# Sharing softmax exponentials between ScalarE and VectorE, and issuing score matmuls more than once

## The chip, the cores and the metric

The kernel runs on one core of a Trainium2 chip. The metric is device time in microseconds of one execution. The engines are TensorE (PE, matmuls), ScalarE (ACT, activations), VectorE (DVE), GpSimd (POOL) and the DMA queues. "Granted clock" is the share of the full TensorE clock that was let through.

## The reference, cut to what matters

```python
# S = 2048 tokens, D = 640, H = 32 heads of Dh = 20, F = 1536
def _A_ref(x, wqkv, wo):                 # attention
    q, k, v = ...                        # x @ wqkv, split into heads
    scores = jnp.einsum("bhqd,bhkd->bhqk", q, k) * (Dh ** -0.5)
    p = _softmax(scores, axis=-1)
    o = jnp.einsum("bhqk,bhkd->bhqd", p, v)
    return o_as_rows @ wo
def _B_ref(x, w1, b1, w2, b2):           # MLP over tokens
    h = _layernorm(x, axis=-1)
    ...
x = x + _A_ref(_layernorm(x), A_wqkv, A_wo)
x = x + _B_ref(_layernorm(x), B_w1, B_b1, B_w2, B_b2)    # layer norm of a layer norm
# ... and both lines once more
```

Per layer 32 heads x 2048 x 2048 exponentials have to be computed, which is 134 million, against 20-column heads that give the matmuls little work.

## The kernel before

Scores are computed transposed, in chunks of 128 keys by 512 queries of one head. Three chunks make a tile of three PSUM banks, and ACT does one exponential over the whole tile. Four heads form a group (64 chunks), and their P V products are accumulated in one bank. Work for other stages (projections, part of the MLP) is "filling": it is issued to PE between tiles.

```python
sps = p1.enter_context(tc.tile_pool(name=f"sps{layer}", bufs=2, space=PSUM))
...
def emit_S(t):
    cs = chunks[3 * t:3 * t + 3]
    ...
    St = sps.tile([128, 3, 512], F32, name="S")
    S_tiles[t] = St
    for i, (n, j) in enumerate(cs):
        s_matmul(St, i, n, j)            # 32-row matmul at row position 32*j

def emit_exp(t):
    ...
    P = ptp.tile([128, 3, 512], BF16, name="P")
    nc.scalar.activation(out=P[:, 0:ncs, :]..., in_=St[:, 0:ncs, :]..., func=ACT.Exp, scale=SCALE)

def emit_PV(n):                          # four chunks, column positions 0, 32, 64, 96
    ...
...
for t in range(NTILES):
    if t + 1 < NTILES:
        emit_S(t + 1)
    emit_exp(t)
    n_pv = 0
    while pv_done < NU and (4 * pv_done + 3) // 3 <= t - LAGT:
        emit_PV(pv_done)
        ...
    emit_fills(CFG["FILL_PV"] if n_pv else CFG["FILL_NOPV"], misc_alloc)
```

The layer norm of a layer norm is done as written, statistics and application twice:

```python
mean, rstd = ln_stats(x1s[:])
t1 = lnw.tile([128, D], F32, name="ln_t1")
ln_apply(t1[:], x1s[:], mean, rstd, engine="dve")
mean2, rstd2 = ln_stats(t1[:])
ln_apply(h2t[:], t1[:], mean2, rstd2, engine="dve")
```

The softmax here doesn't subtract the row's maximum and nothing guards it: scores larger than these inputs give would overflow.

## Time and profile before

Before the prediction there were five runs: median 2176.28 us, 2174.34 to 2180.15.

| stage | from, us | to, us | length, us |
|---|---|---|---|
| prologue | 0 | 50.03 | 50 |
| attention 1 | 50.03 | 1005.68 | 955.7 |
| MLP 1, projections of layer 2 | 1005.68 | 1130.30 | 125 |
| attention 2 | 1130.30 | 2081.30 | 951.0 |
| MLP 2 | 2081.30 | 2174.5 | 93 |

The view of stretches gives the busy time of each engine in the first attention stage of the kernel before (the second has the same, within 1 us for each engine). Its columns are: the stretch, its length, then PE, weight loads, DVE, ACT and POOL busy (with instruction counts), the granted clock, the DMA share and GB/s.

```profile
50.03:1005.68 955.65, 774.35 (x4913) 218.43 (x4912) 216.69 (x423) 927.43 (x683) 67.71 (x96) 0.74 0.12 27
```

ACT is busy for 927 of 956 us and DVE for 217; the granted clock averages 0.74. PE's busy time is measured at a low clock, and the same matmuls take longer there: a group of three score matmuls lasts 0.39 us at 99.80 us, at full clock, and 0.61 at 101.16, at half clock.

### The profile page before, as it was taken

The page shows a single profiled execution, that of the slowest core. Times are in us where ns is not written, and L with a number is a line of the kernel's source. Part 1 is how long each engine was busy: PE and PEld are TensorE (multiplying, and loading weights), DVE is VectorE, ACT ScalarE, POOL GpSimd, SP SyncE. Part 2 cuts the span into 40 slices and gives each one's busy share as a digit, 9 for nine tenths or more (in the row PEclk, how much of TensorE's full clock was granted, in tenths as well). Part 3 has the DMA queues.
Part 4 walks back from the last instruction along what each step waited for, and adds up shares of the span by engine and source line. Part 5 has one row for each costly group of instructions (what it writes and reads, how often), then busy time and mean ns, then how long its engine had stood idle before and what let it go on. Part 6 is the DMA issues. An engine that isn't in the chain of part 4 may idle for free.

```text
span 2174.5 us, 28088 instructions
## 1 busy us (share of the span) xinstructions
PE 1765.4 (81%) x11360; PEld 558.9 (26%) x11360; DVE 584.0 (27%) x1255; ACT 1949.7 (90%) x1508; POOL 166.8 (8%) x250
## 2 busy tenths in 40 slices
PE   7788887777878789886997778788778877898869
PEld 4222222222222122222542222222222221222225
DVE  6112123211421032213642111322123210422242
ACT  5999999999999999995449999999999999999952
POOL 2000000110012001110000000001000110111000
PEclk9877788985887575665999888877668875765569
DMA  5000000110024002223620000101100330122145
GB/s 125 1 1 1 1 10 28 48 63 7 31 56 61 8 28 40 38 31 87 225 84 1 1 1 1 37 20 57 46 25 25 67 57 1 55 47 35 19 135 176
DMA packets 90723, 96.64 MB, mean 44 GB/s; under 512 B 9696, under 2 KB 68192, under 8 KB 90592
## 3 DMA queue, kind: packets, MB, share of 16 engines
q1 hardware_dynamic: 70464, 71.22, 10.5%
q0 software_dynamic: 20128, 23.62, 6.8%
q8 instruction: 89, 1.46, 0.3%
q14 instruction: 42, 0.34, 0.0%
HBM read 55.48 MB, written 39.32 MB: 44 GB/s over the span
## 4 chain that ended last, share of the span: by engine, by line
ACT 43%; PE 32%; issue 21%; DVE 3%; DMA 1%; POOL 0%; ACTq 0%; SPq 0%; DVEq 0%; POOLq 0%
ACT P L312 42%; PE S L293 9%; PE acc L518 5%; PE misc L217 4%; PE y L704 4%; PE misc L393 3%; PE misc L420 2%; PE pp L208 2%; PE misc L453 1%; PE big L633 1%; DMA ua<-uacc 1%; DVE bnst L152 0%; DVE bnst L153 0%; POOL rstd L159 0%; PE pp L217 0%
## 5 line engine op out<-in xcount | busy, mean ns | idle before, releaser
L312 ACT ACTIVATE P<-S 128x1536 bf16<-128x1536 f32 (+1 forms) x1366 | 1854.7, 1538 | 53.0 <-PE S L293 41.8
L293 PE MATMUL S<-QTq,KT 32*128 32x512 bf16 x4096 | 671.4, 481 | 353.2 <-ACT P L312 333.9
L518 PE MATMUL acc<-P,Vaug 128*32 128x512 bf16 x4096 | 513.8, 491 | 5.3 <-DVE T L321 4.1
L293 PEld LDWEIGHTS <-KT 32*128 32x128 bf16 x4096 | 215.8, 94 | 895.2 <-issue 870.6
L518 PEld LDWEIGHTS <-Vaug 128*32 128x32 bf16 x4096 | 111.6, 97 | 336.7 <-issue 336.7
L399 DVE COPY ustg<-misc 128x512 f32<-128x512 f32 (+1 forms) x144 | 70.4, 489 | 348.8 <-PE misc L393 344.3
L393 PE MATMUL misc<-h2st,w1st 128*128 128x512 bf16 (+1 forms) x576 | 155.6, 384 | 0.1
L321 DVE STREAM_TRANSPOSE T<-acc 128x512 f32<-128x512 f32 x64 | 45.8, 716 | 390.8 <-PE acc L518 390.7
L159 POOL TENSOR_TENSOR rstd<-veps,mhalf 128x1 f32<-128x1 f32 x96 | 54.0, 563 | 1222.4 <-DVE veps L157 1195.3
L404 POOL DMA_DIRECT2D uacc<-ustg x96 | 83.0, 866 | 485.6 <-DVE ustg L399 448.2
L217 PE MATMUL misc<-hh,wq_pad 128*128 128x512 bf16 x310 | 119.7, 459 | 0.0
L704 PE MATMUL y<-uT,w2s 128*128 128x512 bf16 (+1 forms) x768 | 107.6, 299 | 2.9 <-ACT uT L647 2.8
L480 DVE CAST QTq<-misc 128x512 bf16<-128x512 f32 x62 | 42.8, 691 | 245.9 <-PE misc L217 245.9
L217 PE MATMUL misc<-hh,wk_pad 128*128 128x512 bf16 x280 | 108.6, 469 | 0.0
L480 DVE CAST KT<-misc 128x512 bf16<-128x512 f32 x56 | 38.7, 691 | 230.8 <-PE misc L217 230.8
L420 PE MATMUL misc<-wo_pad,attnT 128*128 128x512 bf16 (+1 forms) x384 | 95.7, 358 | 0.0
L704 PEld LDWEIGHTS <-w2s 128*128 128x128 bf16 x768 | 59.6, 98 | 49.4 <-issue 4.1
L75 ACT CAST Vaug<-pp 128x500 bf16<-128x500 f32 (+1 forms) x32 | 14.4, 453 | 51.3 <-PE pp L208 51.3
L393 PEld LDWEIGHTS <-w1st 128*128 128x128 bf16 x576 | 38.2, 106 | 73.4 <-issue 71.4
L429 DVE TENSOR_TENSOR x1s<-misc,xin 128x512 f32<-128x512 f32 (+1 forms) x48 | 23.4, 487 | 115.0 <-PE misc L420 114.9
L208 PE MATMUL pp<-wv,hh 128*128 128x500 bf16 (+1 forms) x320 | 50.7, 308 | 1.7 <-DVE hh L77 1.7
L633 PE MATMUL big<-hh 128*128 128x512 bf16 (+2 forms) x192 | 30.9, 326 | 20.5 <-DVE mv L155 19.6
(76 smaller groups left out, 706.3 us busy)
## 6 DMA issues: line engine op xcount, KB each, us to landing
uacc<-ustg POOLq DMA_DIRECT2D x72, 256.0 KB, 3.7
w2s<-in_B_w_dram SPq DMA_DIRECT2D x16, 768.0 KB
w1st<-in_B_w_dram SPq DMA_DIRECT2D x36, 256.0 KB
xd<-x1s SPq DMA_DIRECT2D x24, 320.0 KB
x1in<-xd SPq DMA_DIRECT2D x24, 320.0 KB
ua<-uacc SPq DMA_DIRECT2D x24, 320.0 KB
xd<-x2s SPq DMA_DIRECT2D x16, 320.0 KB
xin<-xd SPq DMA_DIRECT2D x16, 320.0 KB
```

The source lines that it names most:

```text
L159: nc.gpsimd.tensor_tensor(out=rstd[:], in0=veps[:], in1=mhalf[:], op=ALU.pow)
L208: pe(nc.tensor.matmul(pp[:, 0:c1 - c0], lhsT=st.hT[:, dt_, tt * 128:(tt + 1) * 128], rhs=wv[:, dt_, c0:c1], start=(dt_ == 0), stop=(dt_ == ...
L217: pe(nc.tensor.matmul(t[:, :], lhsT=wpad[:, dt_, g, :], rhs=st.hT[:, dt_, tb * 512:(tb + 1) * 512], start=(dt_ == 0), stop=(dt_ == NDT - 1)))
L293: pe(nc.tensor.matmul(St[:, slot, :], lhsT=KT[32 * j:32 * j + 32, g, kt * 128:(kt + 1) * 128], rhs=get_QT(st, qb)[32 * j:32 * j + 32, g, : ...
L312: nc.scalar.activation(out=P[:, 0:ncs, :].rearrange("p a b -> p (a b)"), in_=St[:, 0:ncs, :].rearrange("p a b -> p (a b)"), func=ACT.Exp, ...
L393: pe(nc.tensor.matmul(t[:, 0:w], lhsT=states[fp]["w"][:, sti, ftl * 128:(ftl + 1) * 128], rhs=tiles4[sti][:, c0:c1], start=(sti == 0), sto ...
L399: nc.vector.tensor_copy(out=stg[:, 0:w], in_=t[:, 0:w])
L404: nc.gpsimd.dma_start(out=dst, in_=stg[:, 0:w], accum_op=ALU.add)
L420: pe(nc.tensor.matmul(t[:, 0:w], lhsT=attnT[:, g, ttl * 128:(ttl + 1) * 128], rhs=wo_pad[:, g, c0:c1], start=(g == 0), stop=(g == NG - 1)))
L480: nc.vector.tensor_copy(out=dst_ap, in_=t[:, :])
L518: pe(nc.tensor.matmul(acc[32 * j:32 * j + 32, :], lhsT=Vaug[:, (kt * H + hh) * VW:(kt * H + hh) * VW + 32], rhs=P[:, ci % 3, :], start=(kt ...
L704: pe(nc.tensor.matmul(y[:, 0:w], lhsT=w2s[:, ft, sl * 128:(sl + 1) * 128], rhs=uT[:, ft, c0:c1], start=(ft == 0), stop=(ft == NF - 1)))
```

## The change

The intent has five parts: give some exponentials to DVE, which is mostly idle; split the score buffer so that DVE and ACT can read their parts apart; issue the score matmuls two or three times so that PE stays active and keeps its clock; fold the two layer norms into one; and emit the P V matmuls chunk by chunk from a static model of when each engine will be done, since chunks now become ready in another order. The core of the diff:

```diff
-            sps = ... # [128, 3, 512] tiles, 2 buffers: 6 banks
+            sps = ... # [128, 2, 512] tiles, 2 buffers: 4 banks
+            spsb = p1.enter_context(tc.tile_pool(name=f"spsb{layer}", bufs=2, space=PSUM))
...
-            def emit_S(t):
+            def emit_S(t, passes):
...
-                St = sps.tile([128, 3, 512], F32, name="S")
+                St = sps.tile([128, 2, 512], F32, name="S")
+                St = (St, spsb.tile([128, 512], F32, name="SB"))
                 S_tiles[t] = St
-                for i, (n, j) in enumerate(cs):
-                    s_matmul(St, i, n, j)
+                for _pass in range(passes):
+                    for i, (n, j) in enumerate(cs):
+                        s_matmul(St, i, n, j)
...
+            def want_dve(t):
+                ...                      # position in the head group, 64 chunks
+                if pos > CFG["DVE_LAST"] or pos < 2:          # DVE_LAST = 46
+                    return False
+                return max(clk["dve"] - clk["act"], 0.0) + dve_queued() < CFG["BACKLOG"]   # 2.5
...
+            def emit_tp(t):              # third chunk: scaled copy from PSUM, with a magic constant
+                nc.vector.tensor_scalar(out=batch["tp"][:, i, :], in0=St[1][:], scalar1=SCALE * LOG2E * 128.0,
+                                        scalar2=EXP_MAGIC, op0=ALU.mult, op1=ALU.add)
...
+            # per batch of two chunks: op_frac, op_square, op_lin, op_prod, op_bits
+            #   fraction (int16 -> f16), its square, a linear term, their product,
+            #   and a sum whose int16 bits are the bf16 of exp
...
+                if na == 3:              # a tile without DVE: a second activation for the third chunk
+                    nc.scalar.activation(out=P[:, 2, :], in_=St[1][:], func=ACT.Exp, scale=SCALE)
...
-                    emit_S(t + 1)
+                        on_dve_t[t + 1] = want_dve(t + 1)
+                        emit_S(t + 1, 2 if fill_queue or fill_state["cur"] else 3)
...
-        nc.vector.tensor_scalar_add(out=veps[:], in0=mv[:, 1:2], scalar1=LN_EPS)
+        if twice:                        # 1/sqrt of both norms in one
+            nc.vector.tensor_scalar(out=veps[:], in0=mv[:, 1:2], scalar1=1.0 + LN_EPS, scalar2=LN_EPS * LN_EPS,
+                                    op0=ALU.mult, op1=ALU.add)
```

Cut: the P V bookkeeping by chunk, the queues that place DVE's instructions by hand, and the narrower stride of V (24 to 22 columns).

## The prediction

> **What bounds the kernel now.** I read the page's busy shares first, then the groups by line, then the chain, then short stretches of the timeline.
>
> ```profile
> PE 1765.4 (81%) x11360; PEld 558.9 (26%) x11360; DVE 584.0 (27%) x1255; ACT 1949.7 (90%) x1508; POOL 166.8 (8%) x250
> ...
> PEclk9877788985887575665999888877668875765569
> ...
> ACT 43%; PE 32%; issue 21%; DVE 3%; DMA 1%; POOL 0%; ACTq 0%; SPq 0%; DVEq 0%; POOLq 0%
> ...
> L312 ACT ACTIVATE P<-S 128x1536 bf16<-128x1536 f32 (+1 forms) x1366 | 1854.7, 1538 | 53.0 <-PE S L293 41.8
> L293 PE MATMUL S<-QTq,KT 32*128 32x512 bf16 x4096 | 671.4, 481 | 353.2 <-ACT P L312 333.9
> L518 PE MATMUL acc<-P,Vaug 128*32 128x512 bf16 x4096 | 513.8, 491 | 5.3 <-DVE T L321 4.1
> ```
>
> ACT is busy 90% of the span, 1854.7 of its 1949.7 us in the softmax exponentials. DVE is at 27%. PE waits 333.9 us for the exponentials, so in the two attention stages ACT is the bound. The PEclk line says the granted TensorE clock is far from full there. The timeline gives the stages: exponentials from 50.03 to 1005.68 us and from 1130.30 to 2081.30 us (955.7 and 951.0); the other 268 us are prologue, token MLP and hand-over.
>
> The next stretch shows the rhythm of one tile (three 512-column chunks of scores) and how the clock falls:
>
> ```profile
> 98.46 0.39 PE L293 MATMUL S<-QTq,KT 32*128 32x512 bf16 x3 [0.63 <-ACT P L312]
> 98.78 0.40 PE L518 MATMUL acc<-P,Vaug 128*32 128x512 bf16 x4
> 99.80 0.39 PE L293 MATMUL S<-QTq,KT 32*128 32x512 bf16 x3 [0.62 <-ACT P L312]
> 100.12 0.40 PE L518 MATMUL acc<-P,Vaug 128*32 128x512 bf16 x4
> 100.46 0.77 PE L217 MATMUL misc<-hh,wq_pad 128*128 128x512 bf16 x2
> 101.16 0.61 PE L293 MATMUL S<-QTq,KT 32*128 32x512 bf16 x3
> ```
>
> A tile takes 99.80-98.46 = 1.34 us when ACT sets the pace, against 3x512 elements at 1.2 per ns = 1.28, so 0.063 us is fixed per exponential. Start to start, a score group costs PE 0.32 us and a PV group of four 0.33. After two tiles in which PE sat idle 0.6 us each, the group lengthens from 0.39 to 0.61: the clock has halved. What that costs:
>
> ```profile
> 70.00:76.00 6.00, 4.12 (x33) 1.46 (x30) 0.69 (x1) 6.00 (x6) 0.00 (x0) 1.00 0.00 0
> 80.00:90.00 10.00, 9.08 (x51) 2.09 (x48) 3.75 (x6) 8.27 (x7) 0.00 (x0) 0.64 0.00 0
> 480.00:537.00 57.00, 43.93 (x255) 11.16 (x251) 4.75 (x8) 56.86 (x43) 0.00 (x0) 0.50 0.00 1
> ```
>
> At full clock ACT is busy 6.00 of 6; where the clock is down and PE also has projections to fill in, ACT starves (8.27 of 10); where the clock is down and there is no filling, ACT still gets by (56.86 of 57). Floor per layer: 682x1.343+0.92 = 917 us; measured 956 and 951, so 73 us in both layers are lost, nearly all with the clock down.
>
> [...] taking the granted clock of the first attention in steps of 0.5 us, its 92 changes all fall on one grid of 3.41 us. I added up the streaming time of the matmul groups in each grid window: a full-clock window was followed by half clock when 0.30 to 0.46 of it was streaming (46 windows), and the clock stayed up at a median of 0.52 (90 windows); half clock ended after 0.74 to 0.96 (45 windows). [...] here the fixed part shows 63 ns, which I use. [...] No record before shows the new forms[...].
>
> **The change part by part**, counted in the changed program's instruction order, per layer.
>
> Exponentials. The score buffer is split into a pair and a single bank. [...] ACT now has 683 activations of 1024 columns and 484 of 512; 198 chunks go to DVE. ACT: 683x(0.853+0.063) + 484x(0.427+0.063) = 625.6 + 237.0 = 863 us, against 917. So 84 us of elements leave and 30 us of fixed cost come back: 54 us a layer, 108 in all. That is small because only 198 of 2048 chunks move.
>
> DVE. Each moved chunk is read from PSUM (0.69 us); 96 batches of two then need five dependent operations of 1024 columns: [...] and 0.03 between dependent ones as between the transposes and the multiply now: 3.86. So 5.25 us a batch, 504 a layer, and some 19 for 6 single ones. Gone is the second LayerNorm pass: 12 tiles x (2x0.49+0.20+0.15+0.61) = 23 us. DVE goes from 217 to about 713 us in a stage of 900: 79%, still not the bound on average.
>
> PE. The score matmuls are issued two or three times over: 1543 passes instead of 683. This repeats work with no new result; I take its purpose to be keeping the clock up. Where two score groups follow each other (49.54 us, six matmuls, next group at 50.08) the second costs 0.216. At full clock: scores 683x0.32 + 860x0.216 = 405; PV in 493 bursts, 189 of which need an extra round as two chunks of one head quarter meet: 163+41 = 204; projections as now, 177. Sum 786 us against ACT's 863. Streaming share: with no filling 3 passes + about one PV round = 3.9x0.213 in 1.27 us = 0.65; with filling 2+1+1.1 groups, 0.68. Both are above any window that lost the clock, so I expect the clock to stay near 1.0 and the 73 us of losses to go.
>
> Hand-over to the MLP. The doubled LayerNorm is folded into one (the variance constants combine), so PE's first MLP matmul, now 9.1 us after the last residual add (1015.83 to 1024.90), waits for one chain of statistics instead of two: about 5 us less in each layer, 10 in all.
>
> What is new as loss. (a) A tile with its chunk on DVE takes ACT only 0.92 us, but PE needs 0.54+0.33+0.54 = 1.41 where it also fills. By hand for tiles 192 and 193, both on DVE and both with filling, counting from the end of exponential 189: exponential 191 ends at 2.83, 192 at 3.75. Scores 193 start 0.1 us after the end of 191, at 2.93, and are ready 0.61 later; with PV and filling PE is free at 2.93+1.41 = 4.34, so scores 194 start there and not at 3.85, and are ready at 4.95, while exponential 193 ended at 4.67. ACT waits 0.28 us. A lone 1.41 us tile after it catches nothing up, it only stops the growth. About 60 of 101 such pairs meet filling: 17 us. (b) [...] its work is crowded into the first 46 of 64 chunks of each head group: three batches 15.7 + normalisation 2.4 + five evacuations 3.5 = 21.6 us in about 18.6 us. If the 3 us surplus were paid by PE and ACT in each of 32 groups it would be 96 us a layer; the next 18 chunks drain it and the buffers take a part, so I charge a quarter, 25. (c) start and end of the stage 3. Sum 863+45 = 908 a layer.
>
> Total: 2x908 + 268 - 10 = 2074; I say 2072 us, 4.8% less.
>
> **The rivals.**
> 1. TensorE becomes the bound because the repeats do not hold the clock. For it: the PE sum of 786 is 91% of ACT's. At the present mean clock of 0.74 it would be 1060 us a layer, and the whole near 2380. Against it: streaming shares of 0.65 and more[...]. I give it 3%.
> 2. DVE sets the pace: case (b) paid in full. Its new operations could also be slower than I worked out[...]. Then about 2x(863+17+96+3)+258 = 2216 at the very worst, more likely 2100 to 2150: within 2%. For it: [...] one bank for projections. Against it: the program's own schedule spreads the operations.
> 3. All losses vanish: 2x863+258 = 1984. Against it: PE needs 1.41 us in many 0.92 us tiles.
>
> **Range and chances.** From nearly hidden losses (some 20 a layer: 2x883+258 = 2024) to those of rival 2 at about two thirds (2130): 2025 to 2130. The border for 2% is about 2133. Faster 0.87, within 2% 0.11, slower 0.02.
>
> **What will show it.** Granted clock: 0.95 or more over the attention stages, and no window like 480 to 537 us. ACT: 1366 pair activations and 968 single ones, about 1726 us in start-to-start time, still the busiest engine. PE busy above 90% there. DVE near 72% of the span, its batch of five at 3.9 us. ACT's idle time before exponentials: some 80 to 100 us in all, released by score matmuls. First MLP matmul about 4 us after the last residual add. I am wrong if the clock still falls often, if score matmuls wait for DVE's reads of the single bank for more than 60 us, or if a 512-column activation costs much over 0.49 us.

## The result, and the profile after

The changed kernel takes 2067.30 us (median of 9 runs, 2065.44 to 2071.93) against 2179.21. The ratio is 0.9489, with a 95% interval of 0.9473 to 0.9505. Ratios here are the mean time of one kernel's runs over that of the other's of the same rounds, so they are not quite the ratio of the medians. Where experiments are compared, the ratio is the better measure, because the kernel before differed by up to 10 us; 1% of it is 21.8 us.

From the page of the changed kernel: busy shares, granted clock in 40 slices, the shares of the chain of work that ended last, and the groups that answer to those shown of before. In a group's line, the figures after the bar are busy us, mean ns of one, and the idle time before it with what ended most of it.

```profile
PE 1958.7 (95%) x16522; PEld 596.5 (29%) x16522; DVE 1462.5 (71%) x2511; ACT 1841.9 (89%) x2472; POOL 157.3 (8%) x218
...
PEclk9999999999999999998999999999999999999989
...
PE 55%; ACT 29%; DVE 10%; issue 5%; DMA 1%; POOL 0%; SPq 0%; DVEq 0%; ACTq 0%; POOLq 0%
...
L440 ACT ACTIVATE P<-S 128x1024 bf16<-128x1024 f32 x1366 | 1432.4, 1074 | 59.9 <-PE SB L341 55.3
L341 PE MATMUL S<-QTq,KT 32*128 32x512 bf16 x6176 | 954.7, 380 | 17.9 <-ACT P L440 9.6
L341 PE MATMUL SB<-QTq,KT 32*128 32x512 bf16 x3082 | 883.8, 376 | 20.6 <-ACT KT L84 0.4
L444 ACT ACTIVATE P<-SB 128x512 bf16<-128x512 f32 x968 | 626.3, 647 | 0.0
```

Three things are to be seen. The clock line is full throughout. PE waits for ACT only 9.6 us before score matmuls, where it waited 333.9 us before: the relation has turned, and PE is 55% of the chain that ended last (32% before). The row of pair activations says who ACT still waits for: 55.3 us for the score matmuls into the single bank. And these are not held up by DVE's reads of that bank, which the prediction named as a danger: all idle time before them is 20.6 us.

The same stretches as in the table, in the changed kernel, and the one stretch without filling that the prediction showed at half clock:

```profile
48.94:954.52 905.58, 872.07 (x7494) 236.34 (x7490) 661.00 (x1071) 875.38 (x1167) 65.91 (x84) 0.99 0.13 28
1074.46:1978.75 904.29, 870.59 (x7496) 236.49 (x7496) 660.99 (x1071) 875.10 (x1168) 65.42 (x84) 1.00 0.14 31
480.00:537.00 57.00, 55.73 (x487) 14.93 (x478) 41.67 (x65) 55.37 (x75) 0.00 (x0) 1.00 0.03 9
```

The attention stages shrink by 50.1 and 46.7 us, the rest from 268 to 255.7. ACT's busy time falls from 927 to 875 us, and PE's rises from 774 to 872 at full clock, 96% of the stage. ACT's idle time in the stages is about as before (28.2 and 23.7 us then, 30.2 and 29.2 now). Reckoned from the prediction's floors, the two stages before were 917 + 39 and 917 + 34 us, and are now 863 + 43 and 863 + 41. So the floor fell by 54 us a layer, and what is lost above it stayed about the same: it was lost with the clock before, and is lost in another way now: the lines give 30 us of ACT idle a stage, and 12 us of ACT busy above its floor.

From the timeline of the changed kernel, one batch of two chunks on DVE (start, length):

```profile
150.96 0.69 DVE L385 TENSOR_SCALAR s<-tp 128x1024 f16<-128x1024 int16 x1
151.68 0.69 DVE L389 TENSOR_TENSOR q<-s 128x1024 f16<-128x1024 f16 x1
152.40 0.43 DVE L392 TENSOR_SCALAR s<-s 128x1024 f16<-128x1024 f16 x1
152.86 0.69 DVE L396 TENSOR_TENSOR q<-q,s 128x1024 f16<-128x1024 f16 x1
153.59 1.22 DVE L399 SCALAR_TENSOR_TENSOR PD<-tp,q 128x1024 int16<-128x1024 f32 x1
```

From 150.96 to 154.81 it takes 3.85 us; 3.86 had been worked out.

Where ACT waits for the score matmuls is seen in a stretch of the timeline in which two neighbouring tiles have their third chunk on DVE:

```profile
501.10 2.08 ACT L440 ACTIVATE P<-S 128x1024 bf16<-128x1024 f32 x2
...
502.13 0.40 PE L664 MATMUL acc<-P,Vaug 128*32 128x512 bf16 x4
...
502.47 0.38 PE L341 MATMUL SB<-QTq,KT 32*128 32x512 bf16 x1
...
502.91 0.37 PE L341 MATMUL SB<-QTq,KT 32*128 32x512 bf16 x1
...
503.39 1.02 ACT L440 ACTIVATE P<-S 128x1024 bf16<-128x1024 f32 x1 [0.20 <-PE SB L341]
```

ACT is free at 503.18. The first pass of the next scores is complete at 502.85, but the third pass writes the same buffer until 503.28, and ACT starts at 503.39. Here the repeat, which gives no new result, is itself the wait.

### The profile page after: what moved, and what is told of

It is laid out like the page before. It is cut to its first block, busy times and chain, and to the rows that moved or that the text cites.

```text
span 2065.6 us, 40550 instructions
## 1 busy us (share of the span) xinstructions
PE 1958.7 (95%) x16522; PEld 596.5 (29%) x16522; DVE 1462.5 (71%) x2511; ACT 1841.9 (89%) x2472; POOL 157.3 (8%) x218
## 4 chain that ended last, share of the span: by engine, by line
PE 55%; ACT 29%; DVE 10%; issue 5%; DMA 1%; POOL 0%; SPq 0%; DVEq 0%; ACTq 0%; POOLq 0%
ACT P L440 18%; PE S L341 16%; PE acc L664 11%; ACT P L444 10%; PE SB L341 8%; PE misc L230 6%; PE y L937 5%; PE misc L535 3%; PE misc L563 3%; DVE PD L399 2%; PE pp L221 2%; DVE q L396 1%; PE big L866 1%; DVE q L389 1%; DVE tp L426 1%
## 5 line engine op out<-in xcount | busy, mean ns | idle before, releaser
L440 ACT ACTIVATE P<-S 128x1024 bf16<-128x1024 f32 x1366 | 1432.4, 1074 | 59.9 <-PE SB L341 55.3
L341 PE MATMUL S<-QTq,KT 32*128 32x512 bf16 x6176 | 954.7, 380 | 17.9 <-ACT P L440 9.6
L341 PE MATMUL SB<-QTq,KT 32*128 32x512 bf16 x3082 | 883.8, 376 | 20.6 <-ACT KT L84 0.4
L444 ACT ACTIVATE P<-SB 128x512 bf16<-128x512 f32 x968 | 626.3, 647 | 0.0
L426 DVE TENSOR_SCALAR tp<-SB 128x512 f32<-128x512 f32 x396 | 269.8, 685 | 287.3 <-PE SB L341 285.7
L399 DVE SCALAR_TENSOR_TENSOR PD<-tp,q 128x1024 int16<-128x1024 f32 x204 | 243.0, 1191 | 5.5
L396 DVE TENSOR_TENSOR q<-q,s 128x1024 f16<-128x1024 f16 x204 | 137.6, 675 | 5.8
L389 DVE TENSOR_TENSOR q<-s 128x1024 f16<-128x1024 f16 x204 | 137.5, 674 | 5.8
L385 DVE TENSOR_SCALAR s<-tp 128x1024 f16<-128x1024 int16 x204 | 133.2, 653 | 1.0
L392 DVE TENSOR_SCALAR s<-s 128x1024 f16<-128x1024 f16 x204 | 85.2, 418 | 5.5
```

What stands on the lines that cost most here:

```text
L341: pe(nc.tensor.matmul(St[0][:, slot, :] if slot < 2 else St[1][:], lhsT=KT[32 * j:32 * j + 32, g, kt * 128:(kt + 1) * 128], rhs=get_QT(st, ...
L389: nc.vector.tensor_tensor(out=q16[:, 0:n_], in0=s16[:, 0:n_], in1=s16[:, 0:n_], op=ALU.mult)
L396: nc.vector.tensor_tensor(out=q16[:, 0:n_], in0=q16[:, 0:n_], in1=s16[:, 0:n_], op=ALU.mult)
L399: nc.vector.scalar_tensor_tensor(out=PD[:, 0:nb, :].rearrange("p a b -> p (a b)").bitcast(I16), in0=tp[:, 0:nb, :].rearrange("p a b -> p ( ...
L426: nc.vector.tensor_scalar(out=batch["tp"][:, i, :], in0=St[1][:], scalar1=SCALE * LOG2E * 128.0, scalar2=EXP_MAGIC, op0=ALU.mult, op1=ALU.add)
L440: nc.scalar.activation(out=P[:, 0:nab, :].rearrange("p a b -> p (a b)"), in_=St[0][:, 0:nab, :].rearrange("p a b -> p (a b)"), func=ACT.Ex ...
```

## The experiments

All twelve kernels passed the comparison with the reference; each was timed in 3 rounds beside the kernel before. Diffs of the kernels named "before" are against the kernel before, all others against the changed kernel. The texts say which theory expects what; the main one is the prediction's account, the rivals are that the repeats were not needed, that DVE's delay makes the loss, and that a different buffer would have been better.

### Repeats alone, in the kernel before

```diff
-            def emit_S(t):
+            def emit_S(t, passes=1):
-                for i, (n, j) in enumerate(cs):
-                    s_matmul(St, i, n, j)
+                for _pass in range(passes):
+                    for i, (n, j) in enumerate(cs):
+                        s_matmul(St, i, n, j)
-                    emit_S(t + 1)
+                    emit_S(t + 1, 2 if fill_queue or fill_state["cur"] else 3)
```

> The kernel before with nothing but the repeats (scores issued twice with filling, three times without). Theory A: granted clock over 0.95 in the attention stages, ACT at its floor of 917 us a layer plus some 10: 2 x 927 + 268 = 2122 us, 2.5% under the kernel before. Theory B: the repeats change nothing or add to PE's work: 2175 us or more.

Measured: 2116.31 us (2110.36 to 2125.00) against 2176.67, ratio 0.9722 [0.9689, 0.9756]. Its clock line and its row of exponentials:

```profile
PEclk9999999999999999988999999999999999999989
...
L313 ACT ACTIVATE P<-S 128x1536 bf16<-128x1536 f32 (+1 forms) x1366 | 1837.2, 1726 | 9.9 <-PE S L293 9.4
```

The clock averages 0.981 instead of 0.763, and the idle time before exponentials falls from 53.0 to 9.9 us. Pure repeated work makes the kernel before 60 us faster. Of the 73 us that the prediction put down to the low clock, most come back. This is more than half of what the whole change gains.

### The folded layer norm alone, in the kernel before

```diff
-                mean, rstd = ln_stats(x1s[:])
-                t1 = lnw.tile([128, D], F32, name="ln_t1")
-                ln_apply(t1[:], x1s[:], mean, rstd, engine="dve")
-                mean2, rstd2 = ln_stats(t1[:])
+                mean, rstd = ln_stats(x1s[:], twice=True)
...
-                ln_apply(h2t[:], t1[:], mean2, rstd2, engine="dve")
+                ln_apply(h2t[:], x1s[:], mean, rstd, engine="dve")
```

> The kernel before with nothing but the folded double LayerNorm. The first MLP matmul follows the last residual add by 3.4 us instead of 9.1, so 11 us less in all: a ratio of 0.995 to before. Rival: the freed 46 us of DVE work also matter, then over 20 us less; or the loads of the partial sums take the place of the wait, then under 5 us.

Measured: 2167.14 us (2163.28 to 2181.84) against 2176.67, ratio 0.9965 [0.9924, 1.0006]. The interval includes 1, so the time alone does not settle it. The trace does for the part it concerns: from the end of the last residual add to the first MLP matmul 3.4 us pass (1011.17 to 1014.59), against 9.1 before. In the changed kernel it is 3.4 us too, from 963.56 + 0.89 = 964.45 to 967.87. The first line is of the kernel before, the second fence of the changed one:

```profile
1024.90 1.44 PE L633 MATMUL big<-hh 128*128 128x512 bf16 x5 [9.78 <-DVE mv L155]
```

```profile
967.87 0.58 PE L866 MATMUL big<-hh 128*128 128x512 bf16 x1 [4.13 <-ACT hh L183]
```

The second chain of statistics is gone, and what PE waits for last is the one application. That this is worth the expected 0.5% in the time is likely but not shown.

### No chunk on DVE, everything else kept

```diff
             def want_dve(t):
+                return False
                 cs = chunks[3 * t:3 * t + 3]
```

> The changed kernel with no chunk sent to DVE; repeats, split score buffer and folded LayerNorm stay. ACT then has 683 pairs at 0.907 us and 682 singles at 0.475, as the changed kernel's trace shows them: 944 us a layer. With the clock up and PE at some 750 us little else is lost: attention 950 a layer, in all 2 x 950 + 256 = 2156 us (2145 to 2175). If the new losses of the changed kernel come from DVE tiles, ACT's wait before pair activations falls from 60 us to under 15. If DVE's share hardly mattered the time would be within 15 us of 2067.

Measured: 2191.39 us (2188.69 to 2196.61) against 2176.67, ratio 1.0067 [1.0040, 1.0094], with the clock at 0.982. The direction was right, the size missed by 35 us. Its row of pair activations:

```profile
L441 ACT ACTIVATE P<-S 128x1024 bf16<-128x1024 f32 x1366 | 1888.9, 1536 | 7.5 <-PE SB L341 7.5
```

ACT's wait before them falls from 59.9 to 7.5 us, as expected if the new waits come from the tiles with a chunk on DVE: with the same repeats and full tiles, PE keeps up. As to the size, the expectation had read the start-to-start times of activations in places where ACT had just caught up, and those are too short. Two stretches of ACT's timeline in this run:

```profile
51.53 1.03 ACT L441 ACTIVATE P<-S 128x1024 bf16<-128x1024 f32 x1
...
52.91 1.06 ACT L441 ACTIVATE P<-S 128x1024 bf16<-128x1024 f32 x1
...
908.00 1.78 ACT L441 ACTIVATE P<-S 128x1024 bf16<-128x1024 f32 x1
908.92 1.35 ACT L445 ACTIVATE P<-SB 128x512 bf16<-128x512 f32 x1
909.41 1.78 ACT L441 ACTIVATE P<-S 128x1024 bf16<-128x1024 f32 x1
```

At first a tile starts every 1.38 us (51.53, 52.91), and each recorded pair activation is 0.03 us longer than the last one, so that their ends are 1.41 us apart from the start (52.56, 53.97). In the second stretch a tile also starts every 1.41 us (908.00 to 909.41), with records of 1.78 and 1.35 that overlap. The time that a record lasts is not the time that it costs. The sustained 1.41 is what the prediction had used (0.916 + 0.490 = 1.406), and 683 such tiles are 962 us, against attention stages of about 965 us here. In the trace of the kernel before, the ends of exponentials that follow one another are 1.343 us apart for 1536 columns (median of 1179) and 0.917 for 1024 (the last tile of each stage). So splitting the tile costs a fixed part of some 0.063 us for each of 1366 tiles, about 86 us in two layers; the runs agree: this kernel is 0.9722 x 0.9965 = 0.9688 without the split and 1.0067 with it, 83 us more. (The P V bookkeeping by chunk, the placing of DVE's instructions by hand and the narrower V are in this figure too; no run separates them.) DVE's exponentials then bring 1.0067 down to 0.9489: 126 us. The four terms are -60 for the repeats, -8 for the layer norm, +83 for the split, -126 for DVE: -111 us, which is 1 - 0.9489 of 2179. The 8 us are not told from zero. These terms hold in this order of steps; what the repeats are worth in the finished kernel is another question, which the next run asks.

### One pass of score matmuls

```diff
-                        emit_S(t + 1, 2 if fill_queue or fill_state["cur"] else 3)
+                        emit_S(t + 1, 1)
```

> The changed kernel with every score group issued once. Theory A (the repeats hold the TensorE clock, and a fallen clock costs time): with no filling the streaming share is 1.9 x 0.213 us in 1.27 us = 0.32, [...] so the mean granted clock in the attention stages drops to 0.70 to 0.85, ACT waits for scores well over 100 us in all instead of 60, and the time is 2110 to 2180 us, about 2140. Theory B (moving exponentials to DVE is what pays, the repeats are ballast): PE has 186 us less to do in each layer, so the time is 2067 us or less, down to 2040.

Measured: 2077.71 us (2076.60 to 2079.18) against 2176.67, ratio 0.9543 [0.9517, 0.9570]. Clock line and row of pair activations:

```profile
PEclk9989898876987576886999898999669975777879
...
L440 ACT ACTIVATE P<-S 128x1024 bf16<-128x1024 f32 x1366 | 1465.8, 1117 | 70.1 <-PE SB L341 67.3
```

Both theories missed: the main one had expected 2110 to 2180, the rival 2067 or less. The clock does fall (0.835), so the repeats do hold it; but holding it is worth 10 us here (12 by ratio) and 60 us in the kernel before. ACT's wait goes only from 59.9 to 70.1 us. Perhaps the repeats cost PE time in just those tiles in which PE is late, and so give back most of what the clock gains. This became the question for the next runs.

### A shorter chain on DVE

```diff
                 def op_lin():
-                    nc.vector.tensor_scalar(out=s16[:, 0:n_], in0=s16[:, 0:n_], ...)
+                    pass
                 def op_prod():
-                    nc.vector.tensor_tensor(out=q16[:, 0:n_], in0=q16[:, 0:n_], in1=s16[:, 0:n_], op=ALU.mult)
+                    pass
```

> Two of the five DVE operations of a batch are left out, so the result is wrong on purpose; order, buffers and all else as changed. Each batch of DVE takes 1.17 us less. Theory A (the prediction's loss b: DVE runs behind in each head group and holds up PE and ACT, 25 us a layer): the waits of PV matmuls for DVE (27 us) vanish, ACT waits less, and the time falls by 20 to 50 us, to 2017 to 2047. Theory B (the losses come from PE, whose repeats, PV and projections fill it): less than 10 us change.

This computes another, cruder exponential. The comparison is no fine test of the exponentials of one chunk in ten. Measured: 2051.50 us (2047.54 to 2052.28) against 2180.24, ratio 0.9401 [0.9373, 0.9429], 19 us below the changed kernel by ratio, between the two expectations (20 to 50, and less than 10). The waits that DVE and PE are named for, in the changed kernel and then in this one (total us, times, longest):

```profile
ACT P L440 <- PE SB L341: 55.3, 151, 2.7
...
PE acc L664 <- DVE PD L399: 27.0, 54, 2.3
```

```profile
ACT P L439 <- PE SB L341: 43.9, 134, 1.8
...
PE acc L663 <- DVE PD L398: 7.0, 12, 1.5
```

PE's wait for DVE's results nearly goes, from 27.0 to 7.0 us, but ACT still waits 43.9 us for score matmuls. What this run removes of DVE's delay is therefore worth about 10 us a layer, and the larger part of ACT's waiting is PE's own work.

### Fewer passes around DVE tiles

```diff
-                        emit_S(t + 1, 2 if fill_queue or fill_state["cur"] else 3)
+                        emit_S(t + 1, (1 if on_dve_t[t + 1] or on_dve_t.get(t) else 2)
+                               if fill_queue or fill_state["cur"] else 3)
```

A tile that has its third chunk on DVE, or follows one, gets one pass instead of two while there is filling; 2612 passes instead of 3086.

> Where there is filling, the scores of a tile that goes to DVE and of the tile after it are issued once instead of twice; 474 of 3086 passes go, 51 us of PE work a layer at full clock. Theory B (PE's repeats are what makes ACT wait): ACT's wait for scores falls from 60 to some 25 us and the time by 20 to 35 us, to about 2040, as the streaming share with filling stays at 0.55 and the clock above 0.95. Theory A: PE was not the cause, less than 10 us change. If single windows lose the clock, about 2067 too, with the clock under 0.93.

Measured: 2044.85 us (2042.38 to 2051.71) against 2180.24, ratio 0.9379 [0.9347, 0.9410], 24 us below the changed kernel by ratio. Its row of pair activations:

```profile
L440 ACT ACTIVATE P<-S 128x1024 bf16<-128x1024 f32 x1366 | 1458.2, 1116 | 46.1 <-PE SB L341 42.5
```

The time is as expected; the clock averages 0.971 (0.988 in the changed kernel), and ACT's wait falls by 14 us, not by the expected 35. So repeats in the tiles where PE is short are a cost, and with the filling there one pass nearly keeps the clock.

### Always two passes

```diff
-                        emit_S(t + 1, 2 if fill_queue or fill_state["cur"] else 3)
+                        emit_S(t + 1, 2)
```

> Two passes everywhere, also where there is no filling. The streaming share there is 2.9 x 0.213 in 1.27 us = 0.49, just above the windows that lost the clock in the kernel before (up to 0.46). If that threshold is right the clock stays over 0.95 and the time is within 6 us of 2067, as ACT sets the pace there in either case. If the third pass was needed, the clock falls in the stretches without filling (as from 480 to 537 us) to near 0.5, and the time is 2070 to 2085.

Measured: 2087.11 us (2083.31 to 2090.32) against 2180.24, ratio 0.9562 [0.9527, 0.9596]: slower than the mix of two and three passes, and not told from one (0.9543; the intervals overlap). Clock line and row, and then a stretch without filling with the scores' timeline in it:

```profile
PEclk9999999976999789997999999999979997899989
...
L440 ACT ACTIVATE P<-S 128x1024 bf16<-128x1024 f32 x1366 | 1429.8, 1075 | 80.6 <-PE SB L341 77.1
```

```profile
480.00:540.00 60.00, 57.88 (x420) 12.53 (x420) 40.22 (x62) 55.38 (x74) 0.00 (x0) 0.79 0.00 1
```

```profile
502.12 0.60 PE L341 MATMUL S<-QTq,KT 32*128 32x512 bf16 x2
...
503.64 0.61 PE L341 MATMUL S<-QTq,KT 32*128 32x512 bf16 x2
```

This is what the second theory said, 2 us above its range: two passes did not hold the clock where there is no filling (0.79 from 480 to 540 us, against 1.00 with three), and at half clock they make a tile take 1.52 us of PE (from 502.12 to 503.64), more than ACT's 1.41, so ACT starves (55.38 of 60 us; the changed kernel has 58.1 there).

It also blurs the border of 0.46 of a window that this expectation took from the kernel before. In the traces of the kernel before and of the changed one, every change of the granted clock, between 1 and 0.5, lies on a grid of 3.41 us, and full matmuls of 512 columns start 0.216 us apart at full clock (the median of 722 and of 1025 pairs in the first attention stage). With each matmul counted 0.216 us from its start and what overlaps counted once, the full-clock windows of the first attention stage split as follows:

| trace | next window | windows | share of the window, range | median |
|---|---|---|---|---|
| kernel before | half clock | 46 | 0.32 to 0.44 | 0.40 |
| kernel before | full clock | 90 | 0.40 to 0.70 | 0.52 |
| changed kernel | half clock | 2 | 0.41 and 0.56 | |
| changed kernel | full clock | 259 | 0.50 to 0.87 | 0.78 |

These shares are an estimate from these two traces, and they show no sharp border. A tile without filling and without DVE takes 1.41 us here. With it the prediction's count gives 2.9 x 0.213 / 1.41 = 0.44 with two passes, among the shares that were followed by half clock before, and 3.9 x 0.213 / 1.41 = 0.59 with three, above all of them. The 0.49 and 0.65 expected for the same cases differ from this because they were divided by a mean tile of 1.27 us.

### One pass with filling, three without

```diff
-                        emit_S(t + 1, 2 if fill_queue or fill_state["cur"] else 3)
+                        emit_S(t + 1, 1 if fill_queue or fill_state["cur"] else 3)
```

> Scores issued once wherever there is filling, three times where there is none. [...] the clock mostly stays (0.92 to 0.97 in all), but falls where filling is thin. PE has 168 passes a layer less than in the lean version. If PE's load is still what ACT waits for: 2030 to 2045. If falls of the clock cost more than the spared passes gain: 2045 to 2065.

Measured: 2071.83 us (2069.29 to 2074.42) against 2174.30, ratio 0.9527 [0.9508, 0.9546], the clock at 0.926. Both of its theories missed (2030 to 2045, and up to 2065). It is 0.4% slower than the changed kernel, while the version that keeps two passes in filled tiles away from DVE was 1.1% faster. So the second pass does matter in filled tiles where ACT has all three chunks (the clock was 0.971 with it), and harms around DVE tiles. Its clock line shows where it fell:

```profile
PEclk9999999879999987787999999999999999887789
```

### One three-bank buffer, and one activation for a full tile

```diff
-            spsb = p1.enter_context(tc.tile_pool(name=f"spsb{layer}", bufs=2, space=PSUM))
-                St = sps.tile([128, 2, 512], F32, name="S")
-                St = (St, spsb.tile([128, 512], F32, name="SB"))
+                S3 = sps.tile([128, 3, 512], F32, name="S")
+                St = (S3, S3[:, 2, :])
...
-                nab = min(na, 2)
+                nab = na
...
-                if na == 3:
-                    nc.scalar.activation(out=P[:, 2, :], in_=St[1][:], func=ACT.Exp, scale=SCALE)
```

> One score buffer of three banks again, so that a tile kept on ACT needs one activation of 1536 columns instead of 1024 and 512; chunks to DVE (392), repeats and all else as changed. The fixed 0.063 us of 972 activations go: ACT's floor falls from 863 to 834 us a layer. If ACT's fixed cost was a real price of the split, the time falls by 25 to 55 us, to 2015 to 2040. If the shared buffer costs as much (PE must wait until both ACT and DVE have read, and ACT for all three matmuls), or PE is the bound already, no change or up to 2090.

The split costs fixed time on ACT; can it be had without? Measured: 2106.99 us (2105.10 to 2110.19) against 2180.24, ratio 0.9660 [0.9632, 0.9689], 37 us slower than the changed kernel although ACT has 968 activations fewer, and worse than either expectation (2090 at most). Its row of exponentials and, from the timeline, one place:

```profile
L439 ACT ACTIVATE P<-S 128x1536 bf16<-128x1536 f32 (+1 forms) x1366 | 1710.0, 1341 | 141.9 <-DVE tp L425 126.3
```

```profile
483.50 0.69 DVE L425 TENSOR_SCALAR tp<-S 128x512 f32<-128x512 f32 x1 [4.59 <-PE S L340]
...
484.29 1.02 ACT L439 ACTIVATE P<-S 128x1024 bf16<-128x1024 f32 x1 [0.36 <-DVE tp L425]
```

ACT's exponential of the first two banks starts after DVE has read the third, at 483.50 + 0.69 = 484.19, though neither writes what the other reads. ACT loses 126.3 us in 300 such waits, more than the fixed time saved (968 x 0.063 = 61). With a buffer of its own for the third chunk, both engines read at the same time (in the changed kernel DVE reads it from 500.83 to 501.52 us, and ACT starts on the pair at 501.10): the changed kernel's list of waits has none of pair activations for these reads. Whether the wait comes from the way in which the program keeps track of one buffer is argued from this, not tested by a run of its own.

### More chunks on DVE, with and without the lean passes

Three kernels: the lean rule with `DVE_LAST` 52 (464 chunks on DVE instead of 396), the lean rule with `DVE_LAST` 52 and `BACKLOG` 3.5 (494 chunks), and these two limits without the lean rule.

```diff
-    DVE_LAST=46,
-    BACKLOG=2.5,
+    DVE_LAST=52,
+    BACKLOG=3.5,
```

> The lean version with chunks sent to DVE up to position 52 of 64 in each head group instead of 46: 464 chunks instead of 396. ACT's floor falls by 34 x 0.49 = 17 us a layer, to 846. If ACT is what sets the pace: 2044 - 20 to 30 = 2015 to 2025. If DVE is already near its limit at the end of each group, PV of the next group waits for DVE, and the time stays at 2035 to 2060.

> As the last, with 3.5 us instead of 2.5 us of DVE work allowed to stand in the queue when a chunk is given to DVE: 494 chunks. ACT's floor falls by 24 us a layer against the lean version. DVE would then have some 800 us of work in a stage of 890. If DVE still has room: 2005 to 2020. If it is the new bound: waits of PV for DVE over 100 us, and 2050 to 2090.

> The changed kernel with its repeats as they are and only the two limits on DVE moved (position 52, 3.5 us in the queue): 494 chunks go to DVE. ACT's floor falls by 49 x 0.49 = 24 us a layer, to 839. If the floor of ACT and the work of PE act separately, the time falls by the 45 us that these limits gave on top of the lean version: about 2022. If the repeats' PE work (still 3074 passes) is what holds the tiles that go to DVE, most of it is lost: 2045 to 2070, with ACT waiting 80 us or more for scores.

Measured:

| kernel | median, us (range) | before, us | ratio [95%] | idle before pair activations, us |
|---|---|---|---|---|
| as changed | 2067.30 (2065.44-2071.93) | 2179.21 | 0.9489 [0.9473, 0.9505] | 59.9 |
| lean rule | 2044.85 (2042.38-2051.71) | 2180.24 | 0.9379 [0.9347, 0.9410] | 46.1 |
| limits 52 and 3.5 | 2055.07 (2053.93-2059.06) | 2170.24 | 0.9461 [0.9415, 0.9507] | 84.0 |
| lean rule, limit 52 | 2008.26 (2005.97-2018.13) | 2174.30 | 0.9244 [0.9216, 0.9271] | 50.9 |
| lean rule, limits 52 and 3.5 | 1999.97 (1997.92-2000.69) | 2174.30 | 0.9195 [0.9177, 0.9214] | 45.4 |

The rows of pair activations of the kernel with the limits alone, and then of the kernel with both, whose busy shares stand above it:

```profile
L440 ACT ACTIVATE P<-S 128x1024 bf16<-128x1024 f32 x1366 | 1411.9, 1058 | 84.0 <-PE SB L341 77.6
```

```profile
PE 1819.6 (91%) x14564; PEld 569.2 (28%) x14740; DVE 1685.7 (84%) x2839; ACT 1789.6 (90%) x2374; POOL 157.2 (8%) x218
...
L440 ACT ACTIVATE P<-S 128x1024 bf16<-128x1024 f32 x1366 | 1420.6, 1086 | 45.4 <-PE SB L341 41.1
```

The limits alone came out as their second theory said (2045 to 2070, ACT waiting 80 us or more); the two lean kernels came out 7 and 5 us faster than their best expectation. (The traced execution of the kernel with limit 52 took 2018.13 us, the slowest of its four.) 98 chunks more on DVE take 98 x 0.490 = 48 us off ACT. Alone they gain 0.3%, about 6 us by ratio and not told from zero by the intervals, and ACT's wait for score matmuls grows by 24 us. With the lean rule the same 98 chunks gain 0.9379 - 0.9195 = 1.8%, 40 us, and ACT's wait does not grow. DVE had the room for them in both cases (82 and 84% busy), and PE's wait for DVE's results, 37.7 us with the limits alone, is even longer with both, 48.6; so it is not this wait that held them back, but PE's own work in the shortened tiles. The last kernel beats both: 1999.97 us, 8% under the kernel before. How far it goes is open.

## Why the prediction was right, point by point

**The floor of ACT.** Predicted 863 us a layer from 0.916 and 0.490 us per activation. The sustained 1.41 us per pair and single in the experiment without DVE confirms the sum of the two, the ends in the trace of the changed kernel each of them (a pair after a single ends 0.917 us after it, a single after a pair 0.490, medians of 934 and 968), and the counts (1366 and 968) are those predicted. The two are 0.427 us apart for 512 columns, 1.2 columns per ns, which leaves 0.063 for each activation. It held as a floor; ACT's busy time in a stage is 875 us, 12 above it.

**The clock.** Predicted 0.95 or more in attention, and no more half-clock stretches: 0.99 and 1.00. The reason given, streaming shares of 0.65 and more, was right in its outcome, with a smaller margin than reckoned. It divided by the mean tile of 1.27 us; a full tile without filling takes 1.41, so its share is 0.59, against windows of the kernel before that fell at up to 0.46 by its count, and one of the changed kernel that fell at 0.56 by the count above. Two passes, which the prediction's formula puts at 0.49 and so above those 0.46, lose the clock (0.79 from 480 to 540 us). And half clock lasted: of the 150 half-clock windows in the first attention stage before, 114 lie in spells of 3 to 25 windows, as in the prediction's own line at half clock from 480 to 537 us.

**DVE.** Predicted 79% of a stage or near 72% of the span, a batch at 3.86 us; measured 661 of 905 us or 73% of a stage (52 us less than the 713 reckoned), 71% of the span, 3.85 us. Of its five operations three are recorded with 0.69 us, one with 0.43 and the mixed-width one with 1.22 (150.96 to 154.81 us). No trace of the kernel before shows these forms: the 3.86 was the author's estimate until this trace.

**PE.** Predicted above 90% busy in the stages; measured 96%. It had been counted as 786 us of 863 and so as not quite the bound, and it is nearly one. (The two are not the same measure: a busy time includes the modelled ends of matmuls, 0.38 us each, while the count took 0.216 us a pass.)

**The hand-over.** Predicted about 4 us after the last residual add, and 5 us less a layer; measured 3.4 against 9.1.

**The losses.** Predicted 45 us a layer; measured 905 - 863 = 42. That the sum came out is partly luck, for its terms were off in opposite ways. As waits of ACT, 80 to 100 us had been predicted for both layers, and they are 59.9, 30 a layer; the other 12 us a layer are busy time above the floor, which the prediction did not have and no run explains. The term (b), a quarter of DVE's surplus at 25 us, was too large: with two DVE operations of five left out, the kernel gained 19 us in two layers, about 10 a layer, and PE's wait for DVE was then nearly gone (some delay of the remaining chain may still be in it). The term (a), ACT waiting for PE in DVE tiles at 17 us, was too small: with DVE's chain shortened, ACT still idled 48.5 us in two layers, 24 a layer, released by score matmuls. With 3 us for the ends, 10 + 24 + 3 = 37 of 42; some 5 us a layer no run assigns, and the three are not fully independent.

**What the prediction did not see.** It took the 73 us lost with the clock as a gain of the repeats in the new kernel. In the kernel before that is shown (60 us). In the changed kernel, taking them out costs just 10 us, and with fewer repeats around DVE tiles the kernel gets 24 us faster: PE there is late, and repeats lengthen that. Rival 1 (PE as the bound) was set aside with 3% on the ground of the clock; the clock held, yet PE is what limits further gain, through tiles rather than through the average. Rival 2 (DVE as the pace) came to some 10 us a layer, as far as the shorter chain shows it, and rival 3 (no losses, 1984 us) was not reached by this change, though fewer repeats and more chunks on DVE come to 2000.

## What to carry to other kernels

Before moving work off the busiest engine, ask who has to feed the shortened steps: here 98 more chunks on a VectorE with room to spare gained little until TensorE was relieved in exactly those tiles. Repeated matmuls that hold the clock are a real tool, but they must be enough to hold it (where there was no other work, three passes held it, at 1.00, and two lost it, at 0.79) and must be put where TensorE has slack. When instructions of an engine overlap, read the sustained distance of their starts over a long run (1.41 us a tile here), not the recorded duration (1.78 and 1.35 for its two activations) and not the first few (1.38).
